# Pooling v of batch 0 in two column halves, with all attention loads issued first and half the zero products

## The chip, the cores and the metric

The kernel runs on one core of a Trainium2 chip. The metric is the device time of one execution in microseconds (us); the time of a version is the median over its runs.

## What is computed

An attention over 2 batches and 8 heads (576 tokens, head size 64) is followed by two MLPs over the 1152 tokens. The attention adds a coarse part, over tokens pooled by four, and a local part in which a token sees itself and three neighbours on each side. The second MLP is a sum over four experts, each weighted by a share of the token. All is in float32.

```
q_d, k_d, v_d = mean over 4 tokens of q, k, v
out_up    = repeat(softmax(scale * q_d @ k_d.T) @ v_d, 4)
out_local = softmax(where(|i - j| < 4, scale * q @ k.T, -1e9)) @ v
x = concat_heads(out_up + out_local)                  # 1152 x 512
h = x @ w_in;  x = (h * clip(h + 3, 0, 6) / 6) @ w_out   # 512 -> 2048 -> 512
out = sum over e of p[:, e] * (relu(x @ w1[e]) @ w2[e])  # 512 -> 1024 -> 512
```

## The kernel before

**Stages.** The attention runs in ten rounds, `t` from 0 to 9 (the loop at the end of the functions printed below). A unit is two heads of one batch; units 0 to 3 are batch 0, 4 to 7 batch 1. Each round works on three units at once: the scores of unit `t`, the turned weights of unit `t - 1`, the values of unit `t - 2`. Then the first MLP follows with long products (`three`, lines 382 to 384), and the second MLP (lines 994 and 1273 to 1275). The first four output pieces of the MLP (`early`) already stand in rounds 8 and 9 and right behind.

**A round.** TensorE does, in order: products with zeros (`idle_products`, line 605, whose results nobody reads), the pooled scores (728), the mask (652) and the windowed scores (665), zeros again, the turn of unit `t - 1` (712), the values of unit `t - 2` (802, and 813 for the pooled ones), the pooled turn of unit `t - 1` (782). VectorE takes the row maximum of the pooled scores (`mxd`, 741), that of the windows (`mx`, 682) and the difference (683), the low part of `x` (843), sums and reciprocals (764 to 768, 694, 696), and the sum of both attention parts (`xf`, 827). ScalarE takes the exponentials (753, 689) and copies out of PSUM (719, 720, 790, 821, 835). POOL multiplies by the reciprocals (769, 698) and sums k and q by four for unit `t + 2` (`sums`, 452).

**Banks.** PSUM has three double banks that rotate through the pooled scores, the windowed scores, the turn and the pooled turn, and one called `last` for the values. A pooled turn therefore gets the bank of the same round's pooled scores, once ScalarE has taken the exponentials from it.

**Pooled v.** For batch 0 `pool_v` multiplies v by a matrix of ones (`fours`) in round 1, all 512 columns at once. For batch 1 `load_four` loads the first rows in fours, `add_four` adds them on VectorE (rounds 5 and 6), and `pool_last_v` does the last block on TensorE with a copy by ScalarE (488), in round 5.

**Conversion.** `converting` is a generator that splits blocks of the MLP's weights into a high and a low part. Each call of `convert(1)` runs it to its next `yield`: for block `i` there are four such steps on VectorE, a (line 245), b (255, in two halves), c (267 and 276), d (234). ScalarE's parts are `top_half` (221) and `put_high` (229).

**What sets the order.** Within the attention the engines TensorE, VectorE, ScalarE and POOL run in the order in which the program is written. The loads stand on SyncE's queue. Before, its order is left to a scheduler, and `hold` ties a load to a place in VectorE's order: a memset of one element that the load has to wait for. `later` and `load_next` issue the loads of batch 1 and of the first weight blocks in this way, one in each third of a round. Slots of 8 KB a partition come from a pool (`take`) and go back with `give`.

Of the kernel before, what the change touches and what calls it, by code (L numbers as in the profile page):

```python
# [29 lines left out]
P = 128  # L30
# [83 lines left out]

HELD = 4


IDLE = 11
# [7 lines left out]
def model(ctx: ExitStack, tc: tile.TileContext, qT, kT, v, dp, w_in, w_out, w1, w2, out):  # L126
# [51 lines left out]
    def load_to(n):  # L178
        while loaded[0] <= min(n, len(sources) - 1):
            i = loaded[0]  # L180
            raw[i] = take(order=SHORT)
            if i < HELD:
                hold(raw[i][0])
            nc.sync.dma_start(out=raw[i][0].bitcast(I32), in_=sources[i])
            loaded[0] += 1

    def hold(part):

        nc.vector.memset(part[:1, :1], 0.0)

    def load_half(i, h):
        if h == 0:
            raw[i] = take(order=SHORT)
            loaded[0] = i + 1
        part = slice(h * WT, (h + 1) * WT)
        hold(raw[i][0][:, part])
        nc.sync.dma_start(out=raw[i][0].bitcast(I32)[:, part], in_=sources[i][:, part])

# [189 lines left out]

    def load_k(pair, at=0, n=2, held=False):
# [7 lines left out]
        if held:  # L397
            hold(k[:, 0, FACTOR:])
        nc.sync.dma_start(out=k[:, :, FACTOR - 1 : FACTOR - 1 + S], in_=kT[b, :, hp : hp + n])

    def load_q(pair, at=0, n=2, held=False):
# [4 lines left out]
        if held:  # L406
            hold(q_slots[pair][0])
        for s in range(2):
            nc.sync.dma_start(out=q[:, s], in_=qT[b, s, :, hp : hp + n, :])
# [4 lines left out]

    def v_rows(b, p, p0, first, rows, j0, j1):
        src = v[b, first : first + rows]
        (row, _), (one, _) = src.ap
        nc.sync.dma_start(
            out=v_slots[b][p][0][p0 : p0 + rows, : NJ * DM].rearrange("p (j n) -> p j n", j=NJ)[
                :, j0:j1  # L420
            ],
            in_=bass.AP(src.tensor, src.offset, [[row, rows], [QB * row, j1 - j0], [one, DM]]),
        )

    def load_v(b, p, parts=(0, 1)):
        if 0 in parts:
            v_slots.setdefault(b, []).append(take())
        slot, o = v_slots[b][p][0], FACTOR - 1
        if b and p < 2:
            hold(slot[:, 2 * DM * parts[0] :])  # L430
        if p == 0:
            if 0 in parts:
                nc.vector.memset(slot[:o, :DM], 0.0)
                v_rows(b, p, o, 0, WR, 0, 1)
                v_rows(b, p, WP, WP - o, WP, 0, 1)
                v_rows(b, p, 0, QB - o, P, 1, 2)
            if 1 in parts:
                v_rows(b, p, 0, 4 * QB - o, P, 2, 4)
        elif p == 1:
            for n in parts:  # L440
                v_rows(b, p, 0, (8 + 4 * n) * QB - o, P, 2 * n, 2 * n + 2)
        else:
            at = 16 * QB - o
            nc.vector.memset(slot[QB:W, DM : 2 * DM], 0.0)
            v_rows(b, p, 0, at, WP if b else WR, 0, 1)
            if b:
                v_rows(b, p, WP, at + WP, LAST_ROWS - WP, 0, 1)
            v_rows(b, p, 0, at + QB, QB, 1, 2)
            v_rows(b, p, QB, at + 2 * QB, o, 1, 2)

# [45 lines left out]
    def load_four(part):  # L496

        if part == 0:
            four_slots.append(take())
        to, cols = four(part)  # L500
        hold(to[:, 0])
        nc.sync.dma_start(
            out=to, in_=v[1].rearrange("(p f) d -> p f d", f=FACTOR)[: KR[1][0], :, cols]
        )

    def add_four(part):
# [3 lines left out]
        if part:  # L510
# [4 lines left out]
        tc.manual_schedule(  # L515
            engines={mybir.EngineType.DVE, mybir.EngineType.Activation, mybir.EngineType.Pool}
        )
# [568 lines left out]

    def last_v():
        load_v(1, 1, (1,))
        load_v(1, 2)

    later = [
        lambda: load_half(0, 0),
        lambda: load_half(0, 1),
        lambda: load_v(1, 0, (0,)),
        lambda: load_v(1, 0, (1,)),
        lambda: load_v(1, 1, (0,)),
        last_v,
        lambda: load_k(NU // 2 - 1, held=True),
        lambda: load_q(NU // 2 - 1, held=True),
        lambda: load_four(0),  # L1100
        lambda: load_four(1),
        lambda: load_half(1, 0),
        lambda: load_half(1, 1),
        lambda: None,
        lambda: load_half(2, 0),
        lambda: None,
        lambda: load_half(2, 1),
    ]

    def load_next(t):  # L1110
        if t > 1 and later:
            later.pop(0)()

    make_fours()
    units[0].sums()
    for t in range(NU + 2):
# [5 lines left out]
        if t < NU:  # L1122
# [9 lines left out]
            else:  # L1132
                n.pooled_scores(4)
                n.masks(0)
                n.scores()
                n.pooled_softmax()
                if t == 1:
                    units[0].pooled_normalise()
                    make_last_fours()
                    units[2].sums()  # L1140
                    load_qk(2)
                load_next(t)
                n.less_max()
        if t == NHP + 1:
            pool_last_v()
# [4 lines left out]
        if 0 < t < NU:  # L1150
            n.pooled_normalise()
            n.normalise()
            load_next(t)
        if 0 < t < NU - 2:
# [17 lines left out]
        if t == NHP + 1:  # L1172
            add_four(0)
        convert(3 if t >= NU else 2 if t == 3 else 1 if t > 3 else 0)
        load_next(t)
        if t >= NU:
# [220 lines left out]
```

## Time and profile before

| | |
|---|---|
| median of 3 runs | 652.13 us (651.85 to 654.08) |
| profiled execution, span | 651.4 us (no other time of it is given) |
| TensorE matmul | busy 642.8 us, 99% |
| VectorE | busy 417.8 us, 64% |
| ScalarE | busy 252.7 us, 39% |
| POOL | busy 95.8 us, 15% |
| loads and stores | 46.97 MB, 72 GB/s in the mean |

The span runs from the first to the last instruction of one profiled execution. Busy shares are means over stages that differ; the attention is the first 76 us, and the view that matters is the one cut by round. In the rows PE is TensorE, DVE VectorE, ACT ScalarE and SP SyncE; L728 is line 728 of the kernel before. A row of the timeline gives start, length, engine, line, operation, result and operands with their shapes, how many instructions are merged in it, and in brackets the idle time before it with what ended that. PEclk is the clock granted to TensorE as a share of 2.4 GHz.

### The profile page before, as it was taken

The page shows a single profiled execution, that of the slowest core. Times are in us where ns is not written, and L with a number is a line of the kernel's source. Part 1 is how long each engine was busy: PE and PEld are TensorE (multiplying, and loading weights), DVE is VectorE, ACT ScalarE, POOL GpSimd, SP SyncE. Part 2 cuts the span into 40 slices and gives each one's busy share as a digit, 9 for nine tenths or more (in the row PEclk, how much of TensorE's full clock was granted, in tenths as well). Part 3 has the DMA queues.
Part 4 walks back from the last instruction along what each step waited for, and adds up shares of the span by engine and source line. Part 5 has one row for each costly group of instructions (what it writes and reads, how often), then busy time and mean ns, then how long its engine had stood idle before and what let it go on. Part 6 is the DMA issues. An engine that isn't in the chain of part 4 may idle for free.

```text
span 651.4 us, 11939 instructions
## 1 busy us (share of the span) xinstructions
PE 642.8 (99%) x4909; PEld 581.5 (89%) x4909; DVE 417.8 (64%) x848; ACT 252.7 (39%) x590; POOL 95.8 (15%) x141
## 2 busy tenths in 40 slices
PE   7999999999999999999999999999999999999997
PEld 3556899999999999998898998998998998988986
DVE  6578799962596228595575665665665765765742
ACT  5566576542464235352232233233241341331310
POOL 4753100000000035200201201201201201201000
PEclk9988999999999999999999999999999999999999
DMA  8754424500330110300110110110110210300012
GB/s 260 243 175 148 187 84 138 186 1 1 130 130 0 65 65 1 130 2 1 65 65 0 66 65 0 65 65 2 64 65 1 87 45 0 130 1 1 2 49 97
DMA packets 13368, 46.97 MB, mean 72 GB/s; under 512 B 1385, under 2 KB 4457, under 8 KB 9602
## 3 DMA queue, kind: packets, MB, share of 16 engines
q1 hardware_dynamic: 13314, 46.21, 21.0%
q8 instruction: 38, 0.62, 0.4%
q14 instruction: 16, 0.13, 0.1%
HBM read 43.85 MB, written 2.36 MB: 71 GB/s over the span
## 4 chain that ended last, share of the span: by engine, by line
PE 95%; DMA 2%; DVE 1%; SPq 1%; ACT 0%; issue 0%; POOL 0%; ACTq 0%; POOLq 0%
PE bank L994 27%; PE bank L382 10%; PE bank L383 10%; PE bank L384 10%; PE bank L1273 10%; PE bank L1274 10%; PE bank L1275 10%; PE pair L802 2%; PE pair L605 2%; DMA slot<-in_qT_dram 1%; PE pair L813 1%; DMA slot<-in_v_dram 1%; PE pair L728 1%; PE pair L782 1%; PE pair L665 1%; PE pair L712 0%
## 5 line engine op out<-in xcount | busy, mean ns | idle before, releaser
L994 PEld LDWEIGHTS bank<-xop,slot 128*128 128x128 f32 x1344 | 180.0, 188 | 1.2
L994 PE MATMUL bank<-xop,slot 128*128 128x288 f32 x1344 | 180.8, 295 | 0.0
L1274 PE MATMUL bank<-slot,h 128*128 128x512 f32 x288 | 112.2, 390 | 0.0
L1273 PE MATMUL bank<-slot,h 128*128 128x512 f32 x288 | 112.1, 389 | 0.0
L1275 PE MATMUL bank<-slot,h 128*128 128x512 f32 x288 | 112.1, 389 | 0.0
L1281 DVE SCALAR_TENSOR_TENSOR slot<-bank,pr,slot 128x512 f32<-128x512 f32 x63 | 47.3, 750 | 80.7 <-PE bank L1275 80.7
L452 POOL TENSOR_TENSOR st<-slot 128x256 f32<-128x256 f32 x16 | 13.8, 862 | 462.0 <-DMA slot<-in_w_dram 232.0
L384 PE MATMUL bank<-h,slot 128*128 128x384 f32 x192 | 64.7, 337 | 0.0
L382 PE MATMUL bank<-h,slot 128*128 128x384 f32 x192 | 64.7, 337 | 0.0
L383 PE MATMUL bank<-h,slot 128*128 128x384 f32 x192 | 64.7, 337 | 0.0
L1275 PEld LDWEIGHTS bank<-slot,h 128*128 128x128 f32 x288 | 54.1, 188 | 11.4
L1273 PEld LDWEIGHTS bank<-slot,h 128*128 128x128 f32 x288 | 54.1, 188 | 10.7
L1274 PEld LDWEIGHTS bank<-slot,h 128*128 128x128 f32 x288 | 54.1, 188 | 10.6
L382 PE MATMUL bank<-x,slot 128*128 128x384 f32 x188 | 63.2, 336 | 0.0
L384 PE MATMUL bank<-x,slot 128*128 128x384 f32 x188 | 63.0, 335 | 0.0
L383 PE MATMUL bank<-x,slot 128*128 128x384 f32 x188 | 63.0, 335 | 0.0
L452 DVE TENSOR_TENSOR u<-bank,u 128x288 f32<-128x288 f32 x96 | 43.6, 454 | 20.4 <-PE bank L994 20.0
L1023 ACT ACTIVATE h<-c 128x288 fp32r<-128x288 f32 x64 | 27.7, 445 | 70.8 <-DVE c L452 70.8
L312 ACT ACTIVATE slot<-st 128x512 fp32r<-128x512 f32 x32 | 19.2, 624 | 63.0 <-POOL st L306 63.0
L883 DVE TENSOR_TENSOR h<-slot,h 128x384 fp32r<-128x384 f32 x48 | 27.0, 576 | 24.1 <-ACT h L882 24.0
L874 ACT ACTIVATE t<-bank,half__145 128x384 f32<-128x384 f32 x47 | 27.0, 580 | 38.7 <-PE bank L384 38.5
L875 DVE SCALAR_TENSOR_TENSOR slot<-t,bank 128x384 f32<-128x384 f32 x47 | 25.7, 551 | 24.3 <-ACT t L874 24.1
(121 smaller groups left out, 925.4 us busy)
## 6 DMA issues: line engine op xcount, KB each, us to landing
slot<-in_w_dram SPq DMA_DIRECT2D x16, 1024.0 KB, 4.9
slot<-in_w_out_dram SPq DMA_DIRECT2D x8, 1024.0 KB, 5.0
slot<-in_w_in_dram SPq DMA_DIRECT2D x5, 1024.0 KB, 5.9
slot<-in_v_dram SPq DMA_DIRECT2D x8, 512.0 KB, 5.5
slot<-in_w_in_dram SPq DMA_DIRECT2D x6, 512.0 KB, 4.4
out_dram<-slot SPq DMA_DIRECT2D x9, 256.0 KB, 2.0
slot<-in_kT_dram SPq DMA_DIRECT2D x3, 576.0 KB, 4.4
slot<-in_qT_dram SPq DMA_DIRECT2D x6, 288.0 KB, 5.0
```

Of the source, the lines that this page charges most:

```text
L382: nc.tensor.matmul(ps, wh, xh, start=first, stop=False)
L383: nc.tensor.matmul(ps, wh, xl, start=False, stop=False)
L384: nc.tensor.matmul(ps, wl, xh, start=False, stop=last)
L452: eng.tensor_tensor(out=out, in0=a, in1=b, op=ALU.add)
L874: nc.scalar.activation(out=t, in_=ps, func=AF.Relu, bias=half_, scale=1.0 / (6.0 * UP))
L883: nc.vector.tensor_tensor(out=g[:, 1, :], in0=u, in1=r32(g[:, 0, :]), op=ALU.subtract)
L994: nc.tensor.matmul(ps, a[:, i, k], b[:, j, k], start=start and k == 0 and n == 0, stop=stop and k == 1 and n == 2, skip_group_check=True,)
L1023: nc.scalar.activation(out=self.h[:, 0, i, j], in_=of, func=AF.Relu)
L1273: nc.tensor.matmul(ps, hh, w[:, 0], start=(f == 0), stop=False)
L1274: nc.tensor.matmul(ps, hh, w[:, 1], start=False, stop=False)
L1275: nc.tensor.matmul(ps, hl, w[:, 0], start=False, stop=(f == NF - 1))
L1281: nc.vector.scalar_tensor_tensor(out=to, in0=ps, scalar=share, in1=to, op0=ALU.mult, op1=ALU.add)
```

## The change

- v of batch 0 is loaded and pooled in two halves of 256 columns: the first in round 1 as before, the second in round 3, between the scores and the turn and from one of the rotating banks.
- All attention loads, with the first block of w_in, are issued at the start in order of use, and SyncE's order is the written one. The holds, `later`, `load_half` and `load_next` go. Units are loaded one at a time, q of a unit in one load. The next two blocks of w_in are issued at the end of rounds 2 and 5.
- The zeros ahead of the pooled scores and of the turn are two instead of four, and none ahead of the turn of round 3.
- `pool_last_v` moves from round 5 to round 6. Conversion steps per round: two, one, one, one, one in rounds 3 to 7 before; none, two, one, two, one now.

```diff
-    def hold(part):
-        nc.vector.memset(part[:1, :1], 0.0)
...
     def load_q(pair, at=0, n=2):
...
+        if n == 1:
+            nc.sync.dma_start(
+                out=q[:, :, 0], in_=qT[b, :, :, hp, :].rearrange("s p c -> p s c")
+            )
+            return
...
-    def pool_v(idle):
-        pool = banks(True)
+    def pool_v(pool, idle, cols):
         idle_products(pool, idle)
+        pool = pool[:, :, : DM // 2]
...
-                        v_slots[0][i // 2][0][rows, j * DM : (j + 1) * DM],
+                        v_slots[0][i // 2][0][rows, j * DM + cols.start : j * DM + cols.stop],
...
-            nc.scalar.activation(out=pooled_v(0, kc), in_=pool[: KR[0][kc], kc, :], func=AF.Copy)
+            nc.scalar.activation(
+                out=pooled_v(0, kc)[:, cols], in_=pool[: KR[0][kc], kc, :], func=AF.Copy
+            )
...
+    COLS = (slice(0, DM // 2), slice(DM // 2, DM))
     for p in range(NP):
-        load_v(0, p)
-    load_qk(1)
+        load_v(0, p, cols=COLS[0])
+    load_qk(1, 0, 1)
+    load_qk(1, 1, 1)
+    for p in range(NP):
+        load_v(0, p, cols=COLS[1])
+    for at in range(2):
+        load_qk(2, at, 1)
+    for at in range(2):
+        load_qk(3, at, 1)
+    load_to(0)
+    for p in range(NP):
+        load_v(1, p)
+    for part in range(2):
+        load_four(part)
...
-                n.pooled_scores(4)
+                n.pooled_scores(2)
...
-        if t == NHP + 1:
+        if t == NHP + 2:
             pool_last_v()
...
+        if t == 3:
+            pool_v(banks(), 0, COLS[1])
         if 1 <= t <= NU:
-            units[t - 1].turn(0 if t in (1, NU) else 4)
+            units[t - 1].turn(0 if t in (1, 3, NU) else 2)
...
         if t == 1:
-            pool_v(8)
+            pool_v(banks(True), 8, COLS[0])
...
-        convert(3 if t >= NU else 2 if t == 3 else 1 if t > 3 else 0)
-        load_next(t)
+        convert(3 if t >= NU else {4: 2, 5: 1, 6: 2, 7: 1}.get(t, 0))
+        if t in (2, 5):
+            load_to(loaded[0])
```

SyncE's queue at the start, from the middle of batch 0's v on, before (`slot_98`, `104` and `107` hold its v, `112` and `113` k and q of units 2 and 3):

```order
L418 DMA slot_98<-in_v_dram 128x2x512
L418 DMA slot_104<-in_v_dram 128x2x512 x2
L418 DMA slot_107<-in_v_dram 48x512
L418 DMA slot_107<-in_v_dram 32x512
L418 DMA slot_107<-in_v_dram 3x512
L399 DMA slot_112<-in_kT_dram 128x2x576
L409 DMA slot_113<-in_qT_dram 128x2x288 x2
L409 DMA slot_785<-in_qT_dram 128x2x288
```

The same place now (`slot_96`, `102` and `105` hold the v, `110` and `111` k and q of units 2 and 3):

```order
L402 DMA slot_96<-in_v_dram 128x2x256
L402 DMA slot_102<-in_v_dram 128x2x256 x2
L402 DMA slot_105<-in_v_dram 48x256
L402 DMA slot_105<-in_v_dram 32x256
L402 DMA slot_105<-in_v_dram 3x256
L380 DMA slot_110<-in_kT_dram 128x576
L388 DMA slot_111<-in_qT_dram 128x2x288
```

Half of v's bytes and one unit's k and q now stand ahead of the first sums of unit 2; the other half of v follows behind unit 3.

VectorE at the end of round 6 before, from the last reciprocal to the next round's maximum:

```order
L696 RECIPROCAL rec_1138<-sm_1136 128x10
L189 MEMSET slot_1141 1x1
L827 TENSOR_TENSOR xf_1205<-pair_1162,pd_1203 128x5x64
L827 TENSOR_TENSOR xf_1205<-pair_1162,pd_1203 128x4x64
L234 TENSOR_TENSOR slot_1061<-slot_714,slot_1061 128x512 x2
L741 TENSOR_REDUCE mxd_1274<-pair_1226 72x4
```

The same place now (line 250 and 259 are 267 and 276 of before, 217 is 234, 744 is 741):

```order
L699 RECIPROCAL rec_1135<-sm_1133 128x10
L830 TENSOR_TENSOR xf_1197<-pair_1154,pd_1195 128x5x64
L830 TENSOR_TENSOR xf_1197<-pair_1154,pd_1195 128x4x64
L250 TENSOR_SCALAR slot_902<-slot_902 128x1024
L259 TENSOR_TENSOR slot_902<-slot_902 128x512 x2
L217 TENSOR_TENSOR slot_1216<-slot_902,slot_1216 128x512 x2
L744 TENSOR_REDUCE mxd_1270<-pair_1224 72x4
```

Steps c and d of the first block stand together there; at the end of round 5 step b stands where c stood.

## Rows read from the trace of the kernel before

**Rows 1.** The page, chain of work that ended last, by engine

```profile
PE 95%; DMA 2%; DVE 1%; SPq 1%; ACT 0%; issue 0%; POOL 0%; ACTq 0%; POOLq 0%
```

**Rows 2.** Windows: length, busy us of PE, PEld, DVE, ACT, POOL, PEclk, DMA share, GB/s

```profile
7.91:19.64 11.73, 9.52 (x151) 4.29 (x149) 6.17 (x18) 5.07 (x21) 4.78 (x11) 1.00 0.96 306
...
51.00:59.30 8.30, 8.30 (x191) 5.03 (x189) 7.92 (x21) 5.33 (x17) 2.10 (x4) 0.79 0.36 115
...
75.76:172.20 96.44, 96.44 (x556) 96.34 (x555) 70.93 (x132) 48.61 (x91) 0.00 (x0) 1.00 0.26 94
```

**Rows 3.** Timeline of TensorE, round 1 and the start of round 2

```profile
11.88 0.56 PE L712 MATMUL pair<-ident,ex 64*128 64x64 f32 x10 [0.74 <-POOL ex L698]
...
14.20 1.16 PE L472 MATMUL pair<-slot,fours 38*32 38x512 f32 x8
16.39 2.79 PE L472 MATMUL pair<-slot,fours 38*16 38x512 f32 x28 [1.03 <-DMA slot<-in_v_dram]
...
20.81 0.71 PE L728 MATMUL pair<-slot 64*72 64x144 f32 x8
```

**Rows 4.** Timeline of POOL: sums of q of units 1 and 2

```profile
8.06 1.17 POOL L452 TENSOR_TENSOR slot<-slot 128x288 f32<-128x288 f32 x2 [1.19 <-DMA slot<-in_qT_dram]
...
19.59 1.17 POOL L452 TENSOR_TENSOR slot<-slot 128x288 f32<-128x288 f32 x2 [0.28 <-DMA slot<-in_qT_dram]
```

**Rows 5.** Timeline of TensorE, rounds 4, 5, 7 and the start of 8

```profile
34.05 1.91 PE L605 MATMUL pair<-zeros 128*128 128x512 bf16 x4
35.90 1.24 PE L728 MATMUL pair<-slot 64*72 64x144 f32 x8
...
45.00 1.02 PE L485 MATMUL pair<-slot,last_fours 67*16 67x512 f32 x2
...
48.37 1.35 PE L802 MATMUL pair<-aT,slot 38*64 38x32 f32 x72 [0.86 <-ACT slot L488]
...
60.26 0.71 PE L728 MATMUL pair<-slot 64*72 64x144 f32 x8
...
61.95 1.04 PE L605 MATMUL pair<-zeros 128*128 128x512 bf16 x4
62.91 0.58 PE L712 MATMUL pair<-ident,ex 64*128 64x64 f32 x10
63.43 1.35 PE L802 MATMUL pair<-aT,slot 38*64 38x32 f32 x72
...
65.50 0.72 PE L782 MATMUL pair<-ident,exd 72*128 72x72 f32 x8
66.03 0.42 PE L382 MATMUL pair<-x,slot 128*128 128x384 f32 x1
```

**Rows 6.** Windows of two us, columns as in rows 2

```profile
34.00:36.00 2.00, 2.00 (x9) 0.60 (x9) 1.90 (x4) 1.16 (x3) 1.84 (x4) 0.50 0.70 242
...
46.00:48.00 2.00, 1.51 (x15) 0.71 (x14) 1.86 (x6) 2.00 (x10) 0.20 (x1) 1.00 0.70 224
```

**Rows 7.** Timeline of VectorE, rounds 4 to 7

```profile
43.04 1.75 DVE L255 SCALAR_TENSOR_TENSOR slot<-slot 128x512 f32<-128x512 uint32 x2
44.84 0.75 DVE L741 TENSOR_REDUCE mxd<-pair 72x4 f32<-72x576 f32 x1
...
51.68 1.25 DVE L452 TENSOR_TENSOR slot<-slot 128x512 f32<-128x512 f32 x2
52.85 0.41 DVE L267 TENSOR_SCALAR slot<-slot 128x1024 uint16<-128x1024 uint16 x1
53.30 1.29 DVE L276 TENSOR_TENSOR slot<-slot 128x512 f32<-128x512 f32 x2
...
66.00 0.82 DVE L827 TENSOR_TENSOR xf<-pair,pd 128x320 f32<-128x320 f32 x2 [0.31 <-ACT pd L821]
```

**Rows 8.** Timeline of ScalarE, round 5

```profile
47.34 0.52 ACT L689 ACTIVATE ex<-ex 128x380 f32<-128x380 f32 x1
47.75 0.57 ACT L488 ACTIVATE slot<-pair 16x512 f32<-16x512 f32 x1
```

More of the change, by code (lines that the diff above doesn't have):

```diff
@@ L113 @@
 EARLY = 4
-HELD = 4
 IDLE = 11
@@ L181, in load_to @@
             raw[i] = take(order=SHORT)
-            if i < HELD:
-                hold(raw[i][0])
             nc.sync.dma_start(out=raw[i][0].bitcast(I32), in_=sources[i])
             loaded[0] += 1
-    def hold(part):
-        nc.vector.memset(part[:1, :1], 0.0)
[L191 to L197, printed above, removed]
     def converting():
@@ L387, in model, with load_k @@
     k_slots, q_slots, v_slots = {}, {}, {}
-    def load_k(pair, at=0, n=2, held=False):
+    def load_k(pair, at=0, n=2):
         b, hp = divmod(2 * pair + at, NHP)
@@ L396, in load_k, with load_q @@
             nc.gpsimd.memset(k[:, :, edge], 0.0)
-        if held:
-            hold(k[:, 0, FACTOR:])
         nc.sync.dma_start(out=k[:, :, FACTOR - 1 : FACTOR - 1 + S], in_=kT[b, :, hp : hp + n])
-    def load_q(pair, at=0, n=2, held=False):
+    def load_q(pair, at=0, n=2):
         b, hp = divmod(2 * pair + at, NHP)
@@ L405, in load_q @@
         q = q.rearrange("p (u s c) -> p s u c", u=n, s=2)
-        if held:
-            hold(q_slots[pair][0])
+        if n == 1:
[3 more added lines that the diff above has]
+            return
         for s in range(2):
@@ L413, in load_qk, with v_rows @@
         load_q(pair, at, n)
-    def v_rows(b, p, p0, first, rows, j0, j1):
-        src = v[b, first : first + rows]
-        (row, _), (one, _) = src.ap
+    def v_rows(b, p, p0, first, rows, j0, j1, cols):
+        src = v[b, first : first + rows, cols]
+        (row, _), (one, n) = src.ap
         nc.sync.dma_start(
             out=v_slots[b][p][0][p0 : p0 + rows, : NJ * DM].rearrange("p (j n) -> p j n", j=NJ)[
-                :, j0:j1
+                :, j0:j1, cols
             ],
-            in_=bass.AP(src.tensor, src.offset, [[row, rows], [QB * row, j1 - j0], [one, DM]]),
+            in_=bass.AP(src.tensor, src.offset, [[row, rows], [QB * row, j1 - j0], [one, n]]),
@@ L423, in v_rows, with load_v @@
         )
-    def load_v(b, p, parts=(0, 1)):
-        if 0 in parts:
+    def load_v(b, p, parts=(0, 1), cols=slice(0, DM)):
+        if 0 in parts and cols.start == 0:
             v_slots.setdefault(b, []).append(take())
         slot, o = v_slots[b][p][0], FACTOR - 1
-        if b and p < 2:
-            hold(slot[:, 2 * DM * parts[0] :])
         if p == 0:
             if 0 in parts:
[L433 to L436, printed above, removed]
+                if cols.start == 0:
+                    nc.vector.memset(slot[:o, :DM], 0.0)
+                v_rows(b, p, o, 0, WR, 0, 1, cols)
+                v_rows(b, p, WP, WP - o, WP, 0, 1, cols)
+                v_rows(b, p, 0, QB - o, P, 1, 2, cols)
@@ L437, in load_v @@
             if 1 in parts:
-                v_rows(b, p, 0, 4 * QB - o, P, 2, 4)
+                v_rows(b, p, 0, 4 * QB - o, P, 2, 4, cols)
         elif p == 1:
             for n in parts:
-                v_rows(b, p, 0, (8 + 4 * n) * QB - o, P, 2 * n, 2 * n + 2)
+                v_rows(b, p, 0, (8 + 4 * n) * QB - o, P, 2 * n, 2 * n + 2, cols)
         else:
             at = 16 * QB - o
-            nc.vector.memset(slot[QB:W, DM : 2 * DM], 0.0)
-            v_rows(b, p, 0, at, WP if b else WR, 0, 1)
+            if cols.start == 0:
+                nc.vector.memset(slot[QB:W, DM : 2 * DM], 0.0)
@@ L446, in load_v @@
+            v_rows(b, p, 0, at, WP if b else WR, 0, 1, cols)
             if b:
-                v_rows(b, p, WP, at + WP, LAST_ROWS - WP, 0, 1)
-            v_rows(b, p, 0, at + QB, QB, 1, 2)
-            v_rows(b, p, QB, at + 2 * QB, o, 1, 2)
+                v_rows(b, p, WP, at + WP, LAST_ROWS - WP, 0, 1, cols)
+            v_rows(b, p, 0, at + QB, QB, 1, 2, cols)
+            v_rows(b, p, QB, at + 2 * QB, o, 1, 2, cols)
     def add(eng, out, a, b):
@@ L500, in load_four @@
         to, cols = four(part)
-        hold(to[:, 0])
         nc.sync.dma_start(
@@ L515, in model @@
         tc.manual_schedule(
-            engines={mybir.EngineType.DVE, mybir.EngineType.Activation, mybir.EngineType.Pool}
+            engines={
+                mybir.EngineType.DVE,
+                mybir.EngineType.Activation,
+                mybir.EngineType.Pool,
+                mybir.EngineType.SP,
+            }
         )
@@ L1084, in pieces @@
                 first(*early.pop(0), ps)
[L1087 to L1112, printed above, removed]
     make_fours()
@@ L1140, in model @@
                     units[2].sums()
-                    load_qk(2)
-                load_next(t)
                 n.less_max()
-        if t == NHP + 1:
+        if t == NHP + 2:
             pool_last_v()
@@ L1152, in model @@
             n.normalise()
-            load_next(t)
         if 0 < t < NU - 2:
@@ L1173, in model @@
             add_four(0)
-        convert(3 if t >= NU else 2 if t == 3 else 1 if t > 3 else 0)
-        load_next(t)
+        convert(3 if t >= NU else {4: 2, 5: 1, 6: 2, 7: 1}.get(t, 0))
+        if t in (2, 5):
+            load_to(loaded[0])
         if t >= NU:
```

## The prediction

> **What bounds the kernel now.** I first read the chain that ended last: TensorE holds 95% of it [rows 1], so only a wait of TensorE, or work taken from it, can move the end. Then busy time by stage, cut where TensorE starts a round [rows 2]. From 75.76 to 172.20 us TensorE is busy for the whole 96.44, at full clock, and VectorE for 70.93 of it. The change moves no work into or out of that part, so I expect nothing there. The question is when it starts, and the answer lies in the ten rounds ahead of it.
>
> Two things set the pace of these rounds. In round 1 TensorE waits for data: the pooling of v stops for 1.03 us [rows 3], and the pooled scores of unit 2 start at 20.81 because POOL could sum that unit's q only once it had landed, at 19.59 [rows 3, 4]. From round 2 on TensorE looks busy, but part of that is filler: each round holds two bursts of four products with zeros. In round 7 the steps start at 60.26 (pooled scores), 61.95 (zeros), 62.91 (turn), 63.43 (values), 65.50 (pooled turn), and the next work at 66.03 [rows 5]. A burst of four is 0.96 us, so 0.24 a product; all else is 4.81. VectorE is the other bound: it is busy 7.92 of the 8.30 us of round 6 [rows 2].
>
> **The change, part by part.** I work out S(t), the start of unit t's pooled scores, and from it the start of the first MLP piece, 66.03 before; what that moves forward, the end moves. The profiled execution has a span of 651.4 us and the page gives no other time of it; the median of the runs stands 0.7 above, which I take as what lies around the span. I take the gain off the median.
>
> *Round 1.* The turn at 11.88 waits for POOL's product, behind VectorE's softmax of unit 0 [rows 3]; nothing in that chain moves, so the eight zeros still end at 14.20. Pooling took 2.79 us for 28 matmuls of 512 columns, 0.10 each [rows 3]; 36 of half the columns are 1.8 us if columns set the time, 3.6 if they do not. Has half of v landed by 14.2? The 1.18 MB of k and q of units 0 and 1 had landed by 8.06 and the 2.23 MB of v by 16.39 [rows 3, 4], which is 268 GB/s. Half of v then lands at 12.2, or at 13.0 if its shorter runs move like the four-row loads, at 224 GB/s [rows 6]. No wait, then: pooling ends at 16.0, the pooled turn (0.53) at 16.55, two zeros at 17.05. Unit 2's own 0.59 MB is next in the queue and lands at 14.4 to 15.6; POOL took 1.22 us from there to the scores [rows 3, 4], so it is ready first. With 0.3 of slack S(2) is 17.35 instead of 20.81: **3.5 us**, between 1.7 (half the columns save nothing) and 3.8.
>
> *Rounds 2 to 5.* Round 2 has 4.81 and two bursts of two, 5.77: S(3) = 23.1. Round 3 loses the burst ahead of the turn and gets the second half of the pooling, 4.81 + 1.8 + 0.48 = 7.1: S(4) = 30.2, against 35.90 [rows 5]. Round 4 is 5.77 again: S(5) = 36.0, and by TensorE alone S(6) = 41.75. The gain has grown to 5.7 at S(4).
>
> *Rounds 5 to 7: a wait takes over.* VectorE's order decides here. In round 5 its sum of the values (xf) starts 0.5 us behind TensorE's pooled values, as 66.00 stands to 65.50 [rows 5, 7]: 36.0 + 4.76 + 0.5 = 41.25, where 4.76 is 65.50 - 60.26 less two zeros. Behind xf (0.82) stand the fours (1.17) and now the step of line 255, which has two halves; such steps take 1.29 to 1.75 [rows 7]. With 1.4 unit 6's row maximum starts near 44.65, 2.2 us behind its scores, which TensorE has at 42.4. ScalarE gets to the last pooled block of v only after the exponentials: in round 5 that copy ended 3.48 us after the maximum began (47.75 + 0.57 - 44.84) [rows 7, 8]. This block, with its own matmul of 1.0, now stands in round 6 ahead of the values of unit 4, which need it; they start at 48.2, where TensorE alone would come at 45.4. A wait of 2.8 us takes the place of the 0.86 which the same block (45.00) made in round 5 [rows 5]. From values to the next round is 2.6, two zeros 0.48: S(7) = 51.3, against 60.26.
>
> In round 7 two steps follow xf at 50.75: 0.82, then 0.41 + 1.29, then about 1.75 [rows 7]. Unit 7's maximum starts at 55.0, its exponentials end 2.5 us later (47.34 - 44.84) [rows 7, 8], and only then is the bank of the pooled turn free, which TensorE alone would reach at 56.05: another 1.45. The MLP piece starts at 58.05 instead of 66.03: **8.0 us**. Without these two waits it would be 12.2.
>
> *The clock.* From 34 to 36 us the clock was granted at 0.50, the lower level of 1.2 GHz [rows 6], and round 6 has a mean of 0.79 [rows 2]; the fall at 34.05 comes right behind the stretch from turn to pooled turn, which holds no zeros. Four zeros then took 1.91 instead of 1.04 us, the pooled scores 1.24 instead of 0.71 [rows 5]. Both falls are within the lengths above. With two zeros one costs 0.44 + 0.53 = 1.0. The new waits of rounds 6 and 7 lie in that very stretch, so I expect one fall at 1.0 and, with one chance in two, one that meets the first dense piece: twelve matmuls of 0.173 (96.44 / 556) [rows 2] are 2.1 us and could take twice that. I subtract 2.1; the bounds are 0 and the third rival.
>
> *Transfers and small things.* All attention loads are issued at once, 10.8 MB up to the first four-row load. Counted on from 4.59 MB at 19.59, it lands at 39.9 at the 306 GB/s of round 1 [rows 2], at 42.8 at 268; VectorE wants it at 42.1. I subtract 0.6 for this, between 0 and 5.2 (224 GB/s throughout). The holds that go and two memsets of VectorE, ten more edge memsets of POOL at the start: all of these hide, the former in VectorE's idle time up to 34 us, the latter behind the eleven first zeros. Were that cover gone they would cost about 1 us. The first w_in block stands behind eight loads of k and q and is wanted in round 4: nothing, unless the whole queue is late.
>
> The sum: 8.0 - 2.1 - 0.6 = 5.3; 652.1 - 5.3 = **646.8 us**.
>
> **The rivals.**
> 1. *VectorE does not hold TensorE back*; its backlog is shorter than I count. For: in round 6 VectorE was busy nearly throughout and TensorE had no wait [rows 2]. Against: that round had 8.30 us, and would have 6.8 now. Time: 652.1 - 12.2 + 1.0 = 640.9.
> 2. *The queue is late*: the four-row loads, or unit 2's q, land behind what was put ahead of them, and VectorE or POOL stands still for some 4 us. For: some forty loads are queued from the start. Against: 306 GB/s in round 1 [rows 2]. Time: 646.8 + 4 = 650.8, about no change.
> 3. *The clock stays down*, the other side. Zeros keep TensorE busy between small matmuls; with half of them the stretch without falls below what the chip wants in most rounds. At the lower level a round costs 0.44 for each burst of two, 0.53 for the pooled scores, and for turns and values (3.1 us from 62.91 to 66.03 [rows 5]) between nothing and their whole length again, as no row shows them at that level: 1.4 to 4.5, middle 2.95. It decides from the third such round on, which cancels the 8.0; with six, 652.1 - 8.0 + 17.7 = 661.8. For: two falls even with four zeros [rows 2, 6]. Against: the mean of 0.79 in round 6 says that the clock came back within the round, and zeros remain in both places. The Trainium skill, "TensorE: Matmul & The Clock Gate", section "Why this matters for your kernels", advises against idle gaps between bursts of matmuls, since the clock then returns to its lower rate. By that advice fewer zeros and two new waits bring this rival, and 661.8; by the rows, in which each fall ends, the sum stays at 646.8.
>
> **How the numbers follow.** Forecast 0.62, its own range 644.5 to 649; rival 1 0.11, rival 2 0.17, rival 3 0.10. The range 642.5 to 650.8 leaves out rival 3, most of rival 1 and the worst of rival 2. Half a per cent, about what a measurement of this kernel can tell from no change, is 3.3 us, so the border is 648.8: faster takes rival 1 and most of the forecast (0.68), the same takes rival 2 and the rest (0.22), slower rival 3 (0.10).
>
> **What would show it.** Pooling of v in round 1 near 1.8 us without a wait, and S(2) near 17.4; round 3 near 7.1; in round 6 a wait of the values for ScalarE's copy of the last pooled block, over 2 us; in round 7 a wait of the pooled turn; the first MLP piece between 58 and 61, and the same length from there to the end; two or three dips of the clock. The prediction is wrong if rounds 6 and 7 run without waits (rival 1), if idle time of VectorE or POOL names a DMA (rival 2), or if the clock stays at 0.50 over whole rounds (rival 3).

## The result and the profile after

The changed kernel takes 656.40 us in the median of 9 runs (653.44 to 659.15); the kernel before takes 652.13 us in 9 runs beside them. The ratio is 1.0063, with a 95% interval of 1.0041 to 1.0085: 0.6% slower, where 0.8% faster was forecast. The time lies outside the range, beyond 650.8.

The profiled execution of the changed kernel is its fastest: 653.44 us, a span of 651.7 and a mean granted clock of 0.990. So 1.7 us lie outside the span, not the 0.7 that I took. In the later runs of before, for which both times are known, it is 2.1 to 2.2 us, so its profiled execution, with a span of 651.4 at a clock of 0.995, took some 653.5 us (an estimate) and was not a median run. In 76 later runs of before the medians are 651.61 us and 0.997; the 9 runs of the changed kernel have 0.981. I therefore explain two things: why the two profiled executions are level, where 5.3 us were to be gained, and why the runs of the changed kernel spread upwards from there.

First the timeline of TensorE, rounds 1 to 5 of the changed kernel (pooled scores are line 731 now, scores 668, pooling 456, values 805):

```profile
14.27 1.93 PE L456 MATMUL pair<-slot,fours 38*32 38x256 f32 x36
...
17.19 0.71 PE L731 MATMUL pair<-slot 64*72 64x144 f32 x8
...
23.07 0.71 PE L731 MATMUL pair<-slot 64*72 64x144 f32 x8
...
24.67 1.93 PE L456 MATMUL pair<-slot,fours 38*32 38x256 f32 x36
26.55 0.57 PE L715 MATMUL pair<-ident,ex 64*128 64x64 f32 x10
27.05 0.90 PE L805 MATMUL pair<-aT,slot 38*64 38x32 f32 x47
30.44 0.76 PE L805 MATMUL pair<-aT,slot 38*64 38x32 f32 x25 [2.49 <-issue]
31.13 1.42 PE L816 MATMUL pair<-aTd,slot 80*64 80x144 f32 x8
...
34.45 1.24 PE L731 MATMUL pair<-slot 64*72 64x144 f32 x8
...
41.53 0.71 PE L731 MATMUL pair<-slot 64*72 64x144 f32 x8
...
44.09 0.69 PE L668 MATMUL pair<-slot 64*32 64x38 f32 x55 [1.34 <-issue]
...
47.82 0.60 PE L805 MATMUL pair<-aT,slot 38*64 38x32 f32 x11 [0.93 <-issue]
```

Up to 27.9 us everything is as forecast: no wait for v (before: 1.03 [rows 3]), S(2) at 17.19, S(3) at 23.07, 4.5 us ahead of the 27.55 of before. Then TensorE stops in the middle of a run of 72 like matmuls, 47 in, for 2.49 us, and nothing that the profile shows is waited for ("issue"). It does so again in round 5, twice. The timeline of before has S(3), and its only stop of this kind, here:

```profile
27.55 0.71 PE L728 MATMUL pair<-slot 64*72 64x144 f32 x8
...
32.70 0.85 PE L813 MATMUL pair<-aTd,slot 80*64 80x144 f32 x7 [0.35 <-issue]
```

In the changed kernel rounds 6 and 7 go on:

```profile
51.70 1.24 PE L731 MATMUL pair<-slot 64*72 64x144 f32 x8
...
56.99 1.35 PE L805 MATMUL pair<-aT,slot 38*64 38x32 f32 x72 [0.39 <-ACT slot L474]
...
60.14 0.71 PE L731 MATMUL pair<-slot 64*72 64x144 f32 x8
...
64.70 0.86 PE L816 MATMUL pair<-aTd,slot 128*64 128x144 f32 x8 [0.47 <-issue]
...
66.10 0.44 PE L365 MATMUL pair<-x,slot 128*128 128x384 f32 x1
```

The first MLP piece starts at 66.10, where before had 66.03 [rows 5]: of the lead of 4.5 us nothing is left. From there to the end of the span both profiled executions take the same, 585.6 us here and 585.4 before, so whatever was lost was lost ahead of the first piece. The waits of TensorE from 20 to 70 us, grouped (total, times, longest), here of the changed kernel:

```profile
PE pair L805 <- issue: 3.4, 2, 2.5
PE pair L668 <- issue: 1.3, 1, 1.3
PE pair L816 <- issue: 0.5, 1, 0.5
PE pair L805 <- ACT slot L474: 0.4, 1, 0.4
```

and of before:

```profile
PE pair L802 <- ACT slot L488: 0.9, 1, 0.9
PE pair L813 <- issue: 0.4, 1, 0.4
```

The stops named issue have grown from 0.4 to 5.2 us. The windows of the changed kernel (columns as in rows 2) show what came with them:

```profile
22.00:30.00 8.00, 5.94 (x187) 4.39 (x186) 4.43 (x11) 4.68 (x17) 6.27 (x10) 1.00 1.03 343
30.80:37.70 6.90, 6.90 (x117) 3.97 (x109) 2.28 (x5) 2.46 (x9) 0.66 (x2) 0.51 1.07 285
37.70:47.90 10.20, 7.92 (x261) 5.72 (x262) 7.35 (x19) 7.08 (x24) 5.11 (x7) 1.00 0.80 280
47.90:54.70 6.80, 6.80 (x112) 4.12 (x112) 4.41 (x9) 1.74 (x5) 3.27 (x6) 0.50 0.33 137
```

Behind the first stop, and behind the third, the clock stood at 0.50, the level of 1.2 GHz, for 6.9 and 6.8 us. Before had 3.4 us of it twice (34.0 to 37.4 [rows 6] and 51.0 to 54.4). And in the first two of these stretches, up to 37.7 us, the DMA engines had no free time (share 1.03 and 1.07).

Those two columns led to the theories. **A**: TensorE's instructions are themselves fetched by the DMA engines, and come late when data is queued ahead of them. The page of the changed kernel has a queue for them (q1 carries the data):

```profile
q1 hardware_dynamic: 14120, 46.21, 21.2%
q8 instruction: 38, 0.62, 0.4%
```

38 packets of 0.62 MB are 16 KB each. TensorE has 4917 matmuls and 4917 weight loads; divided by 38 that is 259 instructions a packet. Counted along TensorE's order, the stops at 30.44, 44.09, 47.82 and 64.70 come at instructions 1217, 1729, 1985 and 2754, that is 512, 256 and 769 apart: they stand at borders between blocks of 256 instructions. The DMA view of two stretches of the changed kernel, 24.0 to 27.9 us and 27.8 to 29.3, says when the packet of the first stop came:

```profile
q1 hardware_dynamic: 564, 1.53, 104.8%
```

```profile
q1 hardware_dynamic: 185, 0.38, 94.8%
q8 instruction: 1, 0.02, 4.6%
```

TensorE entered the block ahead at 24.4 us. No instruction packet moved until 27.9, while 1.53 MB of loads did; it ran from 27.93 for 1.1 us, and TensorE went on 1.4 us after its end. **C**: the rest is the clock, which falls behind such stops. **B**, the rival to A: the halves of the pooling, their small matmuls and the fewer zeros stop TensorE themselves.

### The profile page after: what moved, and what is told of

The parts are those of the page before. It is cut to its first block, busy times and chain, and to the rows that moved or that the text cites. A ratio compares the mean times of both kernels' runs of the same rounds, so it can differ in the third digit from the quotient of the medians.

```text
span 651.7 us, 11936 instructions
## 1 busy us (share of the span) xinstructions
PE 639.1 (98%) x4917; PEld 582.0 (89%) x4917; DVE 418.6 (64%) x833; ACT 252.4 (39%) x592; POOL 94.9 (15%) x147
## 3 DMA queue, kind: packets, MB, share of 16 engines
HBM read 43.85 MB, written 2.36 MB: 71 GB/s over the span
## 4 chain that ended last, share of the span: by engine, by line
PE 97%; DVE 1%; issue 1%; ACT 0%; POOL 0%; ACTq 0%; POOLq 0%
PE bank L997 27%; PE bank L365 10%; PE bank L367 10%; PE bank L366 10%; PE bank L1250 10%; PE bank L1249 10%; PE bank L1251 10%; PE pair L608 2%; PE pair L805 2%; PE pair L816 1%; PE pair L668 1%; PE pair L785 1%; PE pair L731 1%; PE pair L715 1%; PE pair L456 1%
## 5 line engine op out<-in xcount | busy, mean ns | idle before, releaser
L886 DVE TENSOR_TENSOR h<-slot,h 128x384 fp32r<-128x384 f32 x48 | 27.6, 586 | 24.1 <-ACT h L885 24.0
```

The source lines that it names most:

```text
L886: nc.vector.tensor_tensor(out=g[:, 1, :], in0=u, in1=r32(g[:, 0, :]), op=ALU.subtract)
```

## The experiments

"Issue" below is the sum of those waits between 20 and 70 us, read from the profile of each version; the medians are over a version's runs, and each ratio is to runs of before taken beside them.

| run | what it is | median us | ratio to before, 95% | median clock | issue us |
|---|---|---|---|---|---|
| before | | 651.61 | 1 | 0.997 | 0.4 |
| after | the change | 656.40 | 1.0041 to 1.0085 | 0.981 | 5.2 |
| e1 | after, four zeros | 657.16 | 1.0051 to 1.0119 | 0.989 | 3.2 |
| e2 | after, later loads spread | 652.52 | 0.9997 to 1.0039 | 0.984 | 3.8 |
| e3 | after, both | 654.02 | 1.0013 to 1.0052 | 0.992 | 3.9 |
| e4 | before, two zeros | 650.94 | 0.9978 to 1.0044 | 0.992 | 1.7 |
| e5 | after, 3.1 MB not loaded | 653.20 | 1.0002 to 1.0038 | 0.986 | 1.7 |
| e6 | before, halves | 655.12 | 1.0027 to 1.0058 | 0.991 | 1.3 |
| e7 | before, loads first | 656.42 | 1.0037 to 1.0084 | 0.992 | 3.8 |
| e8 | before, halves, two zeros | 655.33 | 1.0037 to 1.0101 | 0.984 | 5.0 |
| e12 | e2, zeros for a wait | 653.52 | 1.0006 to 1.0056 | 0.988 | 4.3 |

A wait of 0.20 to 0.36 us beside a burst of zeros that shows one zero too few is not a stop but a missing record (the page of e5 has 4904 matmuls for 4917 weight loads). Without these waits e5 has 0.9 us, e6 1.0, e7 3.6, e8 3.7 and e12 4.0; the others stay.

**e1, e4: the zeros.** In e1 the change keeps four zeros; in e4 the kernel before gets two.

```diff
-                n.pooled_scores(2)
+                n.pooled_scores(4)
...
-            units[t - 1].turn(0 if t in (1, 3, NU) else 2)
+            units[t - 1].turn(0 if t in (1, 3, NU) else 4)
```

> The changed kernel with four zeros again ahead of the pooled scores and of the turn. Theory of the fetch (TensorE's instructions come by DMA in pieces of 16 KB and come late behind the queued loads; in the changed kernel TensorE stood still for 2.49, 1.34, 0.93 and 0.47 us): the zeros only fill part of the stalls, a round is longer by up to 1 us but the stalls get shorter, the sum of the waits named issue stays over 2 us, and the time stays at 653 to 658. Theory of the clock (too few zeros, so that the lower level comes in more rounds): the clock of the runs goes back from 0.978-0.990 to 0.993 or more and the time to 649 to 651.

> The kernel before with two zeros instead of four, all else as it was. Theory of the fetch: its loads are spread, so the instructions come in time; zeros removed shorten rounds 2 to 7, bounded by VectorE: 647 to 651, clock as before. Theory of the clock: falls in more rounds, clock of the runs under 0.99, time 653 to 658.

With four zeros the change is no faster (657.16), and a stop of 2.45 us stands at 30.88; two zeros alone do before no harm that can be measured. So the fewer zeros are not the cause of the loss. But the clock tells that leaving them out isn't free either. Four pairs differ in the zeros alone: before and e4, e1 and after, e3 and e2, e6 and e8. Two zeros have the lower median clock in each, by 0.005, 0.008, 0.008 and 0.007. The median clock of the change is 0.016 below that of before; with four zeros, in e1, it is 0.008 below, so about half goes with the zeros. The median time moved by -0.9, -0.8, -1.5 and +0.2 us, less than the intervals are wide, although 24 to 26 zeros of 0.24 us, about 6 us, were gone. The 12 runs of e4 fall into eight of 649.7 to 653.9 at a clock of 0.991 or more and four of 655.0 to 657.5 at 0.984 or less.

**e2, e3: the traffic.** All loads behind unit 5 are tied to places in VectorE's order, one in each third of a round, as before did it; e3 has four zeros too.

```diff
-    for at in range(2):
-        load_qk(3, at, 1)
-    load_to(0)
-    for p in range(NP):
-        load_v(1, p)
-    for part in range(2):
-        load_four(part)
...
+                load_next(t, 0)
...
+            load_next(t, 1)
...
+        load_next(t, 2)
```

> The changed kernel with two zeros, but the loads behind unit 5 (units 6 and 7, the first block of w_in, v and four-row loads of batch 1) are tied to VectorE's order again, one in each third of a round, so that the queue is not full from 22 to 42 us. Theory of the fetch: the waits named issue on TensorE fall from 5.2 us to under 2, rounds 3 to 5 shorten by 3 us or more, and the time falls to 648 to 652. Theory of the clock: no change in the number of zeros, so the clock stays at 0.978-0.990 and the time at 653 to 658.

> Both edits: loads spread and four zeros. Theory of the fetch: 650 to 653, above the spread kernel with two zeros by what zeros cost without stalls to fill, 1 to 3 us. Theory of the clock: as the four zeros alone, 649 to 651, below the spread kernel with two zeros by 3 us or more.

Spreading gives back 3.9 us of the 4.8 (e2 against after), and 3.1 with four zeros (e3 against e1). This speaks for A, but not all of it came true: the waits stay at 3.8 us where under 2 was expected, e2's 652.5 us lies just above the 648 to 652 expected, and e3's 654.0 above its 650 to 653 (its profile has a stop of 2.80 us at 51.57). In e2 a stop of 2.15 us stays at 30.24, behind loads up to unit 5 that keep the DMA engines busy to 28 us (share 0.91 to 0.97 from 22 us on).

**e5: less traffic.** Batch 1 uses batch 0's first two blocks of v in place of its own, and the two four-row loads are left out; what is left behind unit 5 is spread wider.

```diff
-    for p in range(NP):
-        load_v(1, p)
-    for part in range(2):
-        load_four(part)
+    v_slots[1] = v_slots[0][:2] + [take()]
...
```

> The changed kernel with light traffic: the first two blocks of batch 1's v and the two four-row loads are left out (batch 1 pools and multiplies batch 0's rows in their place), and what is left behind unit 5 (units 6 and 7, the last block of v, the first weights) is spread over rounds 2 to 5. So 3.1 MB of loads are gone from rounds 1 to 5, and the rows of TensorE's order stay the same. Theory A (TensorE's instructions arrive through the same DMA engines as the data, and stand behind the data that is queued): the waits named issue in rounds 3 to 6 fall from 5.2 us to 1 us or less in all, the pooled scores of unit 4 start at 30.5 to 31.5 instead of 34.5, and the time is 645 to 650. Theory B (these stops belong to TensorE's work itself, the halves of the pooling and the fewer zeros, and not to the traffic): stops of 2 us or more stay near 30 us and the time is 653 or more.

The same row of TensorE's order as in the change, in the timeline of e5 (line 848 is the values, 774 the pooled scores):

```profile
27.29 0.90 PE L848 MATMUL pair<-aT,slot 38*64 38x32 f32 x47
28.61 0.66 PE L848 MATMUL pair<-aT,slot 38*64 38x32 f32 x25 [0.42 <-issue]
...
31.19 1.24 PE L774 MATMUL pair<-slot 64*72 64x144 f32 x8 [0.29 <-POOL slot L481]
...
52.02 2.34 PE L848 MATMUL pair<-aT,slot 38*64 38x32 f32 x72 [2.36 <-ACT slot L519]
```

The stop is at the same place, 47 matmuls in, and 0.42 us long instead of 2.49; S(4) comes at 31.19 as A said, instead of 34.45. That part of A holds, and so does its sum: the table has 1.7 us, but 0.9 without the missing records, where A said 1 or less, and only 0.42 and 0.32 of it, at 28.61 and 42.37, stand where the change had its stops of 2.49 and 0.93. The time does not follow: 653.20, where A said 645 to 650. Two things took the place of the stops. In round 6 the values wait 2.36 us for ScalarE's copy of the last pooled block, the wait that I had forecast for the change. And the clock stood at 0.50 for three stretches, together 17 us (30.8 to 34.3, 44.5 to 47.9, 51.3 to 61.6), longer than in the profiled execution of the change with its 5.2 us of stops (13.7). So the clock does not need late instructions to fall. The first piece starts at 64.46 here, 1.6 us ahead of the change.

**e6, e7, e8: one part alone.** In e6 before gets the halves, with its own holds (e8 also two zeros); in e7 it gets the loads first, v undivided and four zeros.

```diff
 e6
+    COLS = (slice(0, DM // 2), slice(DM // 2, DM))
+    for p in range(NP):
+        load_v(0, p, cols=COLS[0])
+    load_qk(1, 0, 1)
+    load_qk(1, 1, 1)
     for p in range(NP):
-        load_v(0, p)
-    load_qk(1)
+        load_v(0, p, cols=COLS[1])
...
+        if t == 3:
+            pool_v(banks(), 0, COLS[1])
 e7
+    for at in range(2):
+        load_qk(3, at, 1)
+    load_to(0)
+    for p in range(NP):
+        load_v(1, p)
+    for part in range(2):
+        load_four(part)
...
-                load_next(t)
```

> The kernel before with one part of the change alone: v of batch 0 loaded and pooled in two column halves, the second in round 3 in place of the zeros ahead of its turn; four zeros elsewhere, and the held loads of before in their places. Theory A (what the halves win in round 1 is lost to late instructions because all loads come first): here the loads behind unit 2 are held, so most of the gain stays: waits named issue under 1.5 us in all, the first MLP piece 2 to 4 us earlier than before, time 648 to 650.5. Theory B (the halves themselves cost it: 36 more small matmuls and their weight loads): the first piece no earlier than 65.5, time 652 to 655.

> The kernel before with another part of the change alone: all attention loads emitted first in order of use, no holds; v undivided, four zeros, conversions and the last pooling where before has them. Theory A: waits named issue of 2 us or more in all appear in rounds 3 to 6 and the time is 653.5 to 657, so this part alone makes the kernel slower. Theory B (the order of the loads is harmless; it is the halves and the fewer zeros): time 651 to 653, issue waits under 1 us.

> The kernel before with v in two halves and two zeros instead of four, but with the held loads of before in their places. Theory A: this keeps what rounds 1 to 3 win, with 1 to 2 us given back to the clock: first MLP piece at 61 to 64, time 646 to 650, faster than before and than the changed kernel by 6 us or more. Theory B (halves and fewer zeros make the loss): 653 or more.

e7 does what A says: the loads alone cost 4.8 us, and in its timeline one new stop stands inside a run of matmuls, and the one of before has grown from 0.35 to 2.03 us at the same place, one pooled value in (664 is the scores, 812 the pooled values):

```profile
28.97 0.57 PE L664 MATMUL pair<-slot 64*32 64x38 f32 x41 [1.52 <-issue]
...
34.61 1.42 PE L812 MATMUL pair<-aTd,slot 80*64 80x144 f32 x7 [2.03 <-issue]
```

e6 and e8 go against what I expected of A. The halves are no gain even with the holds of before: 3.5 us slower in e6, with only 1.3 us of stops. In its profiled run the lead is there at S(3) (24.38 against 27.55) and gone at S(4), 35.08 against 35.90; round 3 holds the second half (1.93), a stop of 1.04 and a fall of the clock (30.9 to 37.8). Its first piece is at 64.85, 1.2 us ahead of before's, in a run of 652.29 us that is the fastest of its twelve. In e8 a stop of 2.09 us stands at 32.52, and the clock is at 0.50 from 27.6 to 41.3. A likely reason, not tested: the holds of before were placed for its own pace, and a kernel that reaches round 3 earlier meets the loads of rounds 1 and 2 there. In e6 the DMA engines have no free time from 18 to 29 us (share 0.97 to 1.05), in before a share of 0.29 from 18 to 22 us and 0.94 to 0.99 from there to 30; e6 comes to its stop at 29.17, before to the same place in its instructions at 32.35. The spread loads of e2 follow later, and e2 is 2.8 us faster than e8.

So the halves alone (e6) and the early loads alone (e7) each make the kernel slower, by 3.5 and 4.8 us, and both with the rest of the change by 4.8: the parts do not add up.

**e9, e10: the change again.** No edit; two more profiles of the changed kernel.

> The changed kernel once more, with no edit, for a second profile: the first one had a granted clock of 0.990, and the other runs of it went down to 0.978. Theory C (the time beyond the late instructions is the clock): a run with a clock of 0.978 to 0.983 has three or more stretches at 0.50 between 25 and 70 us, each behind a stop of TensorE, and a time of 656 to 659; one at 0.987 to 0.990 has two, and 653 to 654.5. Rival D (runs differ by something other than the clock, for instance by loads late in the MLP): the stretches at 0.50 are the same two, and the difference lies behind 76 us. The stops named issue come at the same rows of TensorE's order as in the first profile (L805 in round 3, L668 and L805 in round 5).

> The changed kernel a third time, no edit: as the second, to see more of the spread. Theory C: time and clock go together, about 0.4 us of time for each 0.001 of clock; rival D: they do not.

They took 654.51 us at 0.985 and 660.03 at 0.975. The three stops of rounds 3 and 5 stand at the same rows of the order, but the first is longer: 3.29 and 3.47 us. The stretches at 0.50 are three in e9 (29.6 to 39.8, 50.1 to 53.5, 60.3 to 63.7) and four in e10, the last of them 66.0 to 79.7, in the dense products of the MLP. The timeline of e10 there, and its windows:

```profile
65.39 0.96 PE L816 MATMUL pair<-aTd,slot 128*64 128x144 f32 x8 [0.59 <-issue]
66.28 1.22 PE L785 MATMUL pair<-ident,exd 72*128 72x72 f32 x8
67.25 0.67 PE L365 MATMUL pair<-x,slot 128*128 128x384 f32 x1
67.71 0.52 PE L366 MATMUL pair<-x,slot 128*128 128x384 f32 x1
```

```profile
66.00:79.70 13.70, 13.70 (x131) 12.03 (x128) 8.93 (x18) 7.34 (x21) 1.93 (x2) 0.50 0.05 20
79.70:100.00 20.30, 20.30 (x186) 19.61 (x185) 18.16 (x34) 13.85 (x27) 0.00 (x0) 1.00 0.30 105
```

A piece that took 0.17 us a matmul takes 0.32 here. From the first piece to the end of the span e10 takes 591.0 us; in every other profile of these versions that stretch takes 585.4 to 585.8. So e10 loses 5.4 us to the lower clock in the dense products; the rest of its loss, and all of e9's, lies ahead of the first piece (67.25 and 67.22). For one of e10's stretches, from 21.6 us on, the profile names no wait of TensorE in the 10 us ahead of it, against C's "each behind a stop". Over the 11 runs of the changed kernel time and clock go together (correlation -0.93), with 0.43 us for each 0.001 of clock. By that the 0.009 between the profiled execution (0.990) and the median (0.981) would be 3.9 us; measured are 3.0. The spread goes with the clock, as C says; which of the two causes the other a correlation cannot tell, but e10's dense products show that the clock costs time where there is no stop.

**e11: the border moved.** 64 tiny products with zeros stand in the place of three of the eight zeros of round 1, so that TensorE's list is 122 instructions longer.

```diff
         idle_products(pool, idle)
+        for n in range(64 if idle else 0):
+            nc.tensor.matmul(pool[:32, n % 2, :16], zeros[:, :32], zeros[:, :16], start=True, stop=True)
...
-            pool_v(banks(True), 8, COLS[0])
+            pool_v(banks(True), 5, COLS[0])
```

> The changed kernel with 64 tiny matmuls of zeros (16 columns each) put into round 1 in the place of three of its eight zeros, so that TensorE's list of instructions is 122 longer from there on (a matmul and its weight load each), and nothing else. Theory A (instructions come in blocks of 256, and TensorE stops at the border of a block that is late): the stop of round 3 moves 61 matmuls back in the order, from 47 matmuls into the values (L805) to about 4 before the end of the pooling of the second half; there it stays at 1 to 3 us. Theory B (the stop belongs to the values' own operands or banks): it stays at the values, 47 matmuls in.

It took 659.47 us in its one run, at a clock of 0.983, and its page counts 39 packets on q8 where the change has 38. The timeline of e11 (818 is the pooled values, 458 the pooling):

```profile
24.47 0.33 PE L818 MATMUL pair<-aTd,slot 64*64 64x144 f32 x1 [2.48 <-issue]
...
28.97 1.92 PE L458 MATMUL pair<-slot,fours 38*32 38x256 f32 x33
31.65 0.62 PE L458 MATMUL pair<-slot,fours 38*32 38x256 f32 x3 [0.77 <-issue]
```

The stop left the values for the pooling, 3 matmuls ahead of its end where about 4 were expected; its length is 0.77, below the 1 to 3 us expected, probably because the border ahead of it, now in round 2, already cost 2.48. A stop that moves with the count of instructions, and not with an operation, belongs to the list of instructions. This, with e5 and with e7, which has stops without halves and with four zeros, settles A against B for the stops.

**e12: zeros in the place of a wait.** Six zeros directly ahead of the values of unit 4, in e2.

```diff
             pv = banks(True)
+            idle_products(pv, 6 if self.u == NHP else 0)
```

> The version whose loads behind unit 5 are spread (two zeros), with six more zeros directly ahead of the values of unit 4 in round 6, where that version stood 1.53 us for ScalarE's copy of the last pooled block; six zeros are 1.4 us. Theory C (the clock falls behind stops of TensorE, so that work in the place of a stop saves more than the stop): the stretch at 0.50 from 55.9 to 59.4 us is gone, the mean clock rises from 0.984 to 0.987 or more, and the time falls from 652.5 to 650 to 651.5. Rival D (the fall comes from the small matmuls of the round, whether it stops or not): the fall stays and the time is 652.5 or more.

In the timeline of e12 the zeros waited themselves:

```profile
56.05 1.46 PE L652 MATMUL pair<-zeros 128*128 128x512 bf16 x6 [1.54 <-ACT slot L519]
```

They write the one bank `last`, which the last pooled block fills and ScalarE's copy frees. So what holds the values in round 6 is this bank, and the test of C that it was meant to be did not take place: the wait stayed, and the zeros came on top of it. The stretch at 0.50 from 55.9 us on is gone in this profile all the same and the median clock is 0.988, as C said, while the median time, 653.52, is where rival D had it. A stop of 1.54 us with zeros behind it was followed by no fall; one profile cannot tell whether the zeros did that.

No version here beats the kernel before. The two nearest, e4 and e2, have intervals that take in 1. The moves of the last pooled block and of the conversion steps, the other parts of the change, have no run of their own.

## Why the prediction was wrong

*Round 1 and S(3): right.* The pooling took 1.93 us without a wait (1.8 forecast), S(2) is 17.19 (17.35) and S(3) 23.07 (23.1).

*Rounds 3 to 5: the step that failed.* "S(4) = 30.2", "S(5) = 36.0" and "by TensorE alone S(6) = 41.75" count what TensorE has to do and take for granted that it is told in time. Measured are 34.45, 41.53 and 51.70. Round 3 is 11.38 instead of 7.1: 2.49 of it is the stop, and the other 1.8 lies behind it, at the lower clock, where the pooled turn takes 1.18 instead of 0.70 and two zeros 1.06 instead of 0.60. Round 4 is 7.08 instead of 5.77, its first half at the lower clock. Round 5 is 10.17 where TensorE alone was to take 5.77: 2.27 of stops and 2.1 more behind them. In all S(6) is 9.95 us later than by TensorE alone, where 12.2 were the gain without VectorE's waits. The other 2.3 went in round 6, at first still at the lower clock (8.44 where TensorE alone was to take 6.8), and in round 7 (5.96 where 5.3, of it a stop of 0.47).

*Transfers: the right place with the wrong victim.* I had asked of the full queue only whether data comes late, and subtracted 0.6; rival 2 let POOL or VectorE stand still. Neither did: between 11 and 70 us no wait of either names a load. TensorE's instructions were late. The trace of before showed the sign: a wait of 0.35 us named issue at 32.70, inside a run of matmuls, and a queue of instruction packets. I passed over both because they were small. The Trainium skill, "Trainium Architecture — The Big Picture", section "The software stack", lets the instruction streams be brought to the engines when the program is loaded; the rows of q8 disagree, since its 38 packets start between 12.2 and 620.2 us of the span.

*The waits of VectorE in rounds 6 and 7: hidden in one, not shown in the other.* Of the 2.8 us in round 6 came 0.39, of the 1.45 in round 7 nothing. The rows of the changed kernel (830 is xf, 744 the maximum, 785 the pooled turn, 756 the exponentials):

```profile
50.20 0.82 DVE L830 TENSOR_TENSOR xf<-pair,pd 128x320 f32<-128x320 f32 x2 [2.46 <-ACT pd L824]
53.45 0.75 DVE L744 TENSOR_REDUCE mxd<-pair 72x4 f32<-72x576 f32 x1
...
65.58 0.69 PE L785 MATMUL pair<-ident,exd 72*128 72x72 f32 x8
65.58 0.37 ACT L756 ACTIVATE exd<-pair,nm 72x144 f32<-72x144 f32 x1
```

VectorE's steps took what I had counted: unit 6's maximum began 3.25 us behind xf, where I had 3.4. But TensorE took 6.9 us from the end of the pooled values (49.70) to the place of the next values (56.60), where I had 4.65, for the clock stood at 0.50 from 47.9 to 54.7; so it came to the copy only 0.39 us early. In other versions of this order the same wait is 2.36 us (e5), 1.53 (e2) and 1.35 (e1). So that term was right for the kernel that I had in mind. The term of round 7 is shown by no run: the pooled turn starts without a wait at 65.58, as the last of the four exponentials starts, and I had let it wait until that one ends.

*The clock: under-sized.* I subtracted 2.1 us for one fall and half of another, and gave 0.10 to a clock that stays down. In the profiled execution two stretches together have 13.7 us at 0.50 (before 6.8); the median run has about 25 by its clock (an estimate: 0.019 of 654.6, twice). The case that I gave one chance in two, a fall that meets the dense piece, came in e10 with 13.7 us and a loss of 5.4, where I had put 2.1 on it. Rival 3 is the nearest of the rivals to the result, and right in part: missing zeros go with about half of the lower clock (e1 against the change). But the clock did not stay down over most rounds, and with four zeros it fell too. The Trainium skill, "TensorE: Matmul & The Clock Gate", section "Why this matters for your kernels", advises against idle gaps, and I had weighed that less than the rows of before. The order in time agrees with it here, at 30.8 and 47.9 us behind stops of 2.49 and 0.93 us, and the 656.4 measured lies nearer to the 661.8 of that rival than to my 646.8.

What stays open: what makes the clock fall. All but two of the 33 falls in the profiles of these versions came during a wait of TensorE or within 3 us of its end, down to one of 0.31 us in e12; but e10's first has none named in the 10 us ahead of it, the waits of 0.74 and 0.86 us in round 1 were followed by none, and e5, with 0.9 us of stops named issue, had 17 us at 0.50. That waits cause the falls is argued from their order in time; the run meant to test it, e12, did not take the wait away. And how much of e6's 3.5 us is the clock (0.991 against 0.997, some 2.6 us if the 0.43 for 0.001 of the changed kernel holds there) and how much its second half of pooling was not tried apart.

## What to carry to other kernels

A TensorE program of many small matmuls is itself a stream of data: look up the instruction queue in the profile, divide TensorE's instructions by its packets, and where "issue" stands inside a run of like matmuls, see whether the packet came late behind loads. Issuing all loads early is then not free, even when every load is in time. And judge such a kernel by the clock of many runs: one profiled execution at 0.990 hid 3 us that the median at 0.981 had.

## What the runs showed of the hardware

- TensorE's instructions came during the execution in packets of 16 KB, 256 instructions, over the DMA engines that carry the data. A packet took 0.9 to 1.4 us in the change. Under a full queue it started up to 4.5 us after TensorE had entered the block ahead, and behind a stop TensorE went on 1.2 to 1.7 us after its end; the stops were up to 3.5 us (e10).
- Matmuls of 256 columns instead of 512 saved their columns: 36 took 1.93 us, 0.054 each, against 0.10 for 512 [rows 3].
- Zeros taken out of TensorE's filler went with a lower clock: 24 less lowered the median clock by 0.008, and of their 6 us a gain of 0.8 is left, which is not clear of noise (e1 to after).
- The lower clock costs time by itself: 13.7 us of it in the dense products lengthened them by 5.4 us, at 0.32 instead of 0.17 us a matmul (e10).
